# The end of a one-core program: semaphores cleared while the last two stores are in flight, and no release after the clear

## The chip, the cores and the metric

The kernel runs on one core of a Trainium2 chip. A core has five engines that run their own instruction streams: TensorE (PE in the profile), VectorE (DVE), ScalarE (ACT), GpSimd (POOL) and SyncE (SP), and 16 DMA engines that move data between the chip's memory (HBM) and the core's on-chip memory. [...]The number that counts is the device time of one execution in microseconds. It is longer than the span on the profile page, which goes from the first to the last instruction of the program.

## The reference

Two blocks follow each other. The first is a cross-covariance attention over channels, for 4 batches of 6400 tokens with 256 channels; the second is a mixture of 8 low-rank adapters of rank 16, of which each token takes the best two.

```python
qn = q / (norm(q, axis=1) + 1e-6);  kn = k / (norm(k, axis=1) + 1e-6)
a  = softmax(kn.T @ qn / tau)                 # 256 x 256 for each batch
x  = (v @ a).reshape(25600, 256)
logits = x @ w_gate                           # 8 experts
w  = softmax(top2(logits))
out = x + sum over the two experts e of  w_e * (x @ A[e]) @ B[e]
```

## The kernel before

Tokens lie on the 128 partitions, 50 chunks of 128 tokens for each batch. For each batch the kernel first sums the 256x256 matrix `kT q` over all 50 chunks (`do_G`), makes the attention matrix from it, and then goes through the 6400 tokens of `v` in five pieces of ten chunks: transposes, gate logits, the adapter's inner product, and at last the sum `Y` (`do_Y`, lines 955 and 960), which is copied out of the accumulator banks (`do_Ye`, through the copy helper at lines 810 and 812) and stored (`do_store`, line 971).

The order of the instructions on every engine is worked out ahead by a planner (`Plan.run`, with a rank for each step and a simulated clock) and written out as it stands. Loads are issued by GpSimd (line 627), stores by SyncE (line 971). The last two pieces of the last batch are stored in three parts each (`FINE = 2`: four, four and two chunks), so the stores at the end are of 512, 512 and 256 KB, twice. Each store raises one of eight semaphores of SyncE's DMAs by 16 when it is complete; the stores go round these eight in turn. In the built program the store before the last has semaphore 110, the last one has 111, and the one ahead of them 109.

What comes after the last store is the last block of the program, and it is made by the framework, not by the planner. As built and then shortened by `one_end_barrier` (line 487; it edits the list of instructions of that block when the program is finished), it reads:

- SyncE: nine waits (EVENT_SEMAPHORE), each for two semaphores, so that every load, store and engine has come to its last count; then a DRAIN that waits for a tenth and a DRAIN that raises semaphore 96, "gather".
- TensorE, VectorE and ScalarE: a DRAIN that raises semaphore 96, and then a wait for semaphore 97, "release".
- GpSimd: a DRAIN; a wait until semaphore 96 is at four, which takes the four off again; a DRAIN that resets DMA state for the semaphores 99 to 118; one EVENT_SEMAPHORE_RANGE_CLEAR that sets these to zero; a DRAIN; and a raise of semaphore 97 by four, the release.
- All but GpSimd: the wait for semaphore 97, which takes one off, and then the program is over.

All instructions of the block carry line 1030 in the profile, the end of the `with` block that holds the kernel.

Of the kernel before, what the change touches and what calls it, by code (L numbers as in the profile page):

```python
# [486 lines left out]
def one_end_barrier(nc):  # L487


    def trim(nc):  # L490
        end = nc.main_func.blocks[-1]
        ins = list(end.instructions)
        pool = [n for n, i in enumerate(ins) if i.engine == mybir.EngineType.Pool]
        clear = next(n for n in pool if type(ins[n]).__name__ == "InstISA")
        before = [n for n in pool if n < clear and type(ins[n]).__name__ == "InstEventSemaphore"]
        after = [n for n in range(clear + 1, len(ins))]
        release = [n for n in after if n in pool and type(ins[n]).__name__ == "InstEventSemaphore"]
        assert len(before) == 2 and len(release) == 2 and len(after) == 11, (before, release, after)
        drop = {before[-1]} | {n for n in after if n != release[-1] and n != release[0] - 1}
        end.instructions = [i for n, i in enumerate(ins) if n not in drop]  # L500
    nc.at_finalize(trim)


# [1 line left out]
def kernel(  # L505
# [484 lines left out]
    for s in steps:  # L990
        do[s.key[0]](s, *s.key[1:])
        if s.key[0] == "load":
# [3 lines left out]
            if n_load == 4:  # L996
                make_consts()
    first_ahead(nc, {i.ins.name for i in early})
    one_end_barrier(nc)


# [33 lines left out]
```

## Time and profile before

The median of three runs is 254.42 us, the lowest 254.33, the highest 254.62. The profiled run took 254.2 us, with a span of 252.4 us.

| What | before |
|---|---|
| time, us | 254.42 (254.33 to 254.62) |
| span, us | 252.4 |
| TensorE busy | 222.0 us, 88% of the span |
| DMA engines, mean busy share in 38 of the 40 slices | nine tenths or more |
| last matmul ends | about 244.5 us |
| last copy into the output tile | 244.54 to 245.13 us |
| last store issued | 245.15 to 245.65 us |
| last store complete (semaphore 111 at its final count) | 251.51 us |
| last instruction of the program ends | 252.42 us |

The page of the profile gives busy time by engine, the share in 40 slices and the chain of work that ended last. Waits, semaphores, DRAINs and DMA issues are not counted as busy, so the page shows nothing of what happens after the last copy; for that one asks for the instructions of line 1030, for who waited for whom on SyncE, and for the trace's record of single instructions and of semaphore updates with their times. A wait's start in these records is when it was satisfied, not when it began to wait.

### The profile page before, as it was taken

What the parts mean: (1) busy time and instruction counts of PE and PEld (TensorE: products, weight loads), DVE (VectorE), ACT (ScalarE), POOL (GpSimd) and SP (SyncE); (2) the same over time, 40 slices, a digit from 0 to 9 for tenths busy, and PEclk for the clock granted to TensorE, in tenths of its full rate; (3) what the DMA queues carried; (4) which work ended last, traced back from release to release, by engine and by line L of the source; (5) the groups of instructions that cost most, each with busy time, mean ns of one, the idle gap of its engine ahead of it and who ended that gap; (6) DMA issues with size and microseconds to landing.
All of it is one profiled execution on the core that took longest, in us unless ns stands there. A gap on an engine that the chain in (4) does not pass through costs nothing.

```text
span 252.4 us, 6005 instructions
## 1 busy us (share of the span) xinstructions
PE 222.0 (88%) x2467; PEld 196.5 (78%) x2467; DVE 170.8 (68%) x485; ACT 158.1 (63%) x294; POOL 26.8 (11%) x54
## 2 busy tenths in 40 slices
PE   0875995899999899999998997899998989999970
PEld 0463784699899898889996996699977879999960
DVE  0025386179987988777849678869996897598430
ACT  5424223375977758767674778756953958877750
POOL 7003011011000210000102103010000110000000
PEclk9979798599999999999999999999999999999996
DMA  8999999999999999999999999999999999999995
GB/s 255 213 217 209 212 225 210 214 219 216 214 210 235 297 214 220 312 293 235 220 213 314 222 214 218 209 216 210 216 300 407 424 243 300 354 388 430 420 414 219
DMA packets 11147, 66.71 MB, mean 264 GB/s; under 512 B 1264, under 2 KB 1648, under 8 KB 6512
## 3 DMA queue, kind: packets, MB, share of 16 engines
q0 software_dynamic: 6912, 38.80, 74.6%
q1 hardware_dynamic: 3872, 26.87, 25.9%
q10 hardware_dynamic: 336, 0.66, 0.7%
q8 instruction: 19, 0.31, 0.4%
q14 instruction: 8, 0.07, 0.1%
HBM read 78.91 MB, written 26.21 MB: 416 GB/s over the span
## 4 chain that ended last, share of the span: by engine, by line
PE 47%; DMA 37%; DVE 6%; ACT 5%; issue 1%; POOL 0%; POOLq 0%; DVEq 0%
DMA qk<-in_k_dram 25%; PE Y_ps L955 12%; DMA v<-in_v_dram 7%; PE acc L642 7%; PE Y_ps L960 6%; DMA out_dram<-y 5%; PE T_ps L828 5%; PE Z_ps L919 4%; PE gzT_ps L942 4%; PE ZL_ps L852 3%; DVE ssq L670 2%; ACT sq L664 2%; PE acc L646 2%; PE acc L651 2%; PE log_ps L866 1%
## 5 line engine op out<-in xcount | busy, mean ns | idle before, releaser
L642 PE MATMUL acc<-qk 128*128 128x256 bf16 x400 | 74.6, 285 | 14.7 <-DMA qk<-in_k_dram 8.4
L955 PE MATMUL Y_ps<-a_bf,vT 128*128 128x256 bf16 x400 | 60.0, 272 | 0.6 <-ACT y L810 0.6
L670 DVE TENSOR_TENSOR ssq<-ssq,sq 128x1280 f32<-128x1280 f32 (+1 forms) x27 | 43.3, 1603 | 25.3 <-ACT sq L664 25.1
L810 ACT COPY y<-Y_ps 128x512 f32<-128x512 f32 x83 | 47.9, 589 | 18.7 <-PE Y_ps L960 12.0
L664 ACT ACTIVATE sq<-qk 128x1280 f32<-128x1280 bf16 (+1 forms) x27 | 36.9, 1368 | 27.8 <-DVE ssq L670 9.9
L642 PEld LDWEIGHTS <-qk 128*128 128x128 bf16 x400 | 35.8, 103 | 20.3 <-DMA qk<-in_k_dram 10.3
L955 PEld LDWEIGHTS <-vT 128*128 128x128 bf16 x400 | 38.7, 98 | 5.0 <-issue 0.7
L960 PE MATMUL Y_ps<-ball,gzT 128*128 128x256 bf16 x200 | 38.2, 273 | 0.0
L646 PE MATMUL acc<-qk 128*128 128x128 bf16 x210 | 30.4, 227 | 0.0
L651 PE MATMUL acc<-qk 128*128 128x128 bf16 x200 | 28.7, 227 | 0.0
L828 PE MATMUL T_ps<-ident,v 128*128 128x128 f32 x200 | 28.0, 274 | 0.0
L930 DVE TENSOR_TENSOR gz<-Z_ps,gateg 128x256 bf16<-128x256 f32 x60 | 22.4, 439 | 4.2 <-PE Z_ps L919 4.0
L810 ACT COPY vT<-T_ps 128x512 f32<-128x512 f32 (+1 forms) x43 | 21.7, 540 | 5.2 <-PE T_ps L828 4.9
L646 PEld LDWEIGHTS <-qk 128*128 128x128 bf16 x210 | 21.4, 102 | 3.2
L828 PEld LDWEIGHTS T_ps<-ident,v 128*128 128x128 f32 x200 | 21.9, 141 | 0.5
L810 ACT COPY gzT<-gzT_ps 128x256 f32<-128x256 f32 (+1 forms) x45 | 14.7, 348 | 11.9 <-PE gzT_ps L942 11.7
L627 POOL DMA_DIRECT2D v<-in_v_dram x20 | 11.1, 553 | 101.3 <-PE T_ps L828 69.0
L960 PEld LDWEIGHTS <-gzT 128*128 128x128 bf16 x200 | 19.4, 98 | 2.5 <-DVE gzT L812 0.3
L942 PE MATMUL gzT_ps<-ident,gz 128*128 128x128 f32 x100 | 19.7, 281 | 1.4 <-DVE gz L930 1.0
L651 PEld LDWEIGHTS <-qk 128*128 128x128 bf16 x200 | 18.7, 102 | 2.2
L664 ACT ACTIVATE ssq<-qk 128x1536 f32<-128x1536 bf16 x8 | 11.9, 1486 | 9.5 <-DMA qk<-in_k_dram 5.0
L919 PE MATMUL Z_ps<-waA_sb,vT 128*128 128x128 bf16 x240 | 17.7, 219 | 0.0
(80 smaller groups left out, 275.1 us busy)
## 6 DMA issues: line engine op xcount, KB each, us to landing
out_dram<-y SPq DMA_DIRECT2D x18, 1280.0 KB, 13.0
v<-in_v_dram POOLq DMA_DIRECT2D x20, 640.0 KB, 25.6
qk<-in_q_dram POOLq DMA_DIRECT2D x7, 1088.0 KB, 22.9
qk<-in_k_dram POOLq DMA_DIRECT2D x7, 1088.0 KB, 27.5
qk<-in_q_dram POOLq DMA_DIRECT2D x4, 512.0 KB, 23.4
qk<-in_k_dram POOLq DMA_DIRECT2D x4, 512.0 KB, 24.6
qk<-in_q_dram POOLq DMA_DIRECT2D x2, 1024.0 KB, 31.3
qk<-in_k_dram POOLq DMA_DIRECT2D x2, 1024.0 KB, 35.8
```

Of the source, the lines that this page charges most:

```text
L642: nc.tensor.matmul(acc[ic][:, 0:256], kt[:, j, ic::CC], qt[:, j, :], start=c == 0, stop=False, skip_group_check=True)
L646: nc.tensor.matmul(acc[ic][:, 256:384], kt[:, j, ic::CC], kt[:, j, ic::CC], start=False, stop=False, skip_group_check=True)
L651: nc.tensor.matmul(acc[ic][:, 384:512], qt[:, j, ic * P:(ic + 1) * P], qt[:, j, ic * P:(ic + 1) * P], start=False, stop=c == NC - 1, skip_ ...
L664: nc.scalar.activation(out[:, 0:n, :], t[:, j:j + n, :], ACT.Square)
L670: nc.vector.tensor_tensor(out=t, in0=t, in1=held["sq", (w, b, g), ""][:, 0:n, :], op=OP.add)
L810: nc.scalar.copy(out, in_)
L828: nc.tensor.matmul(ps[:, j, :], vt[:, c + j, :].bitcast(FP32), W["ident32"], is_transpose=True, start=(j == 0), stop=(j == n - 1))
L919: nc.tensor.matmul(ps[:, j, :], vT_of(b, i, c + j)[:, :, ic], st[b]["aA"][:, ic, :], start=(j == 0 and ic == 0), stop=(j == n - 1 and ic = ...
L930: nc.vector.tensor_tensor(out=pairs[:, h].rearrange("p c (e r) -> p c e r", e=E), in0=z[:, 2 * h:2 * h + 2, :].rearrange("p c (e r) -> p c ...
L942: nc.tensor.matmul(ps[:, j, :], pairs[:, j * P:(j + 1) * P], W["ident32"], is_transpose=True, start=(j == 0), stop=(j == n // 2 - 1))
L955: nc.tensor.matmul(ps[:, j, :], vT_of(b, i, c + j)[:, :, ic], st[b]["a"][:, ic, :], start=(j == 0 and ic == 0), stop=False, skip_group_che ...
L960: nc.tensor.matmul(ps[:, j, :], pair[:, :, j], W["B"], start=False, stop=(j == 1), skip_group_check=True)
```

## The change

The edit is in `one_end_barrier` alone, so every instruction up to the last store stays as it was. It rebuilds the last block. SyncE's first waits leave out the two semaphores of the last two stores (110 and 111). SyncE then raises the gather semaphore, and only after that waits for 110 and for 111, and takes the count of each off in the same instruction, so that they end at zero. GpSimd's clear is cut into two ranges that leave these two out, 99 to 109 and 112 to 118, each with its DMA reset ahead of it. The release and the waits for it are gone: TensorE, VectorE and ScalarE end after their DRAIN, GpSimd after its second clear. Its purpose is that the clearing lies beside the last two stores instead of behind them.

```diff
+    LATE = 2
+
     def trim(nc):
...
+        copies = [i for i in nc.main_func.blocks[-2].instructions
+                  if i.engine == sp and type(i).__name__ == "InstDMACopy"]
+        late = [i.sync_info.on_update[0].id for i in copies[-LATE:]]
...
+        tail = [step(mybir.InstDrain, sp, [w for w in waits if w.id not in late])]
+        tail += [step(mybir.InstDrain, e, (), signal[e]) for e in signal]
+        for x in late:
+            w = next(w for w in waits if w.id == x)
+            tail.append(step(mybir.InstEventSemaphore, sp, [w], [mybir.SyncUpdate(
+                sync_type="semaphore", id=x, ant_name=w.ant_name, update_mode="sem-sub-imm",
+                update_value=w.wait_value, update_reg=None)]))
+        tail += [ins[[i.engine for i in ins].index(pool)], joined]
...
+        for a, x in spans:
+            n0 = len(end.instructions)
+            nc.gpsimd.dma_reset(range(a, x))
+            nc.gpsimd.sem_clear(range(a, x))
+            tail += list(end.instructions)[n0:]
+        end.instructions = tail
     nc.at_finalize(trim)
```

More of the change, by code (lines that the diff above doesn't have):

```diff
@@ L487, in one_end_barrier @@
 def one_end_barrier(nc):
+    LATE = 2
     def trim(nc):
+        sp, pool = mybir.EngineType.SP, mybir.EngineType.Pool
         end = nc.main_func.blocks[-1]
         ins = list(end.instructions)
[L493 to L500, printed above, removed]
+        copies = [i for i in nc.main_func.blocks[-2].instructions
+                  if i.engine == sp and type(i).__name__ == "InstDMACopy"]
@@ new lines, in trim, with step @@
+        late = [i.sync_info.on_update[0].id for i in copies[-LATE:]]
+        clear = next(n for n, i in enumerate(ins) if type(i).__name__ == "InstISA")
+        lo, hi = ins[clear].ant_dict["range_first"], ins[clear].ant_dict["range_last"]
+        assert len(set(late)) == LATE and all(lo <= x <= hi for x in late)
+        def step(kind, engine, wait=(), update=()):
+            return kind(name=nc.get_next_instruction_name(), engine=engine,
+                        sync_info=mybir.SyncInfo(on_wait=list(wait), on_update=list(update)))
@@ new lines, in trim @@
+        first = next(i for i in ins if i.engine == sp)
+        waits = list(first.sync_info.on_wait)
+        signal = {i.engine: list(i.sync_info.on_update) for i in ins[:clear]
+                  if type(i).__name__ == "InstDrain" and i.engine != pool and i is not first}
+        joined = next(i for i in ins[:clear] if i.engine == pool and type(i).__name__ == "InstEventSemaphore")
+        tail = [step(mybir.InstDrain, sp, [w for w in waits if w.id not in late])]
+        tail += [step(mybir.InstDrain, e, (), signal[e]) for e in signal]
@@ new lines, in trim @@
+        for x in late:
[4 more added lines that the diff above has]
+        tail += [ins[[i.engine for i in ins].index(pool)], joined]
+        spans, a = [], lo
+        for x in sorted(late) + [hi + 1]:
+            if x > a:
+                spans.append((a, x))
+            a = x + 1
```

## The prediction

> **What bounds the end now.** The change touches nothing ahead of the last store, so I read only how the program ends, in four steps. First the slices of the span:
>
> ```profile
> PE   0875995899999899999998997899998989999970
> DMA  8999999999999999999999999999999999999995
> ```
>
> For most of the span both TensorE and the DMA engines are near full; in the last slice (6.3 us) TensorE is idle and DMA is half busy. The last 6 to 7 us belong to stores and to what follows them. The waits of SyncE, over 245.5 to 253 us, say which:
>
> ```profile
> SPq L1030 <- DMA out_dram<-y: 5.6, 5, 2.0
> SPq L1030 <- PEq L1030: 0.5, 1, 0.5
> ```
>
> Columns: waiter, releaser, us in total, times, longest. Five of SyncE's end waits are ended by a store that completes; the sixth, 0.5 us, is a wait at line 1030 itself: SyncE waits for the clear and the release. (The view names PE; by semaphore it is GpSimd's release, 97.) Third, the instructions of line 1030 from 251.45 us to the end: those behind the last store's completion (columns: duration in ns as min/median/max, first and last start):
>
> ```profile
> L1030 SPq EVENT_SEMAPHORE  x5: 17/28/28, 251.5 to 252.4; - x5
> L1030 SPq DRAIN  x2: 7/7/7, 251.8 to 251.8; - x2
> L1030 POOLq EVENT_SEMAPHORE  x2: 17/17/17, 251.9 to 252.3; - x2
> L1030 POOLq DRAIN  x2: 40/66/93, 252.0 to 252.2; - x2
> L1030 POOLq EVENT_SEMAPHORE_RANGE_CLEAR  x1: 139/139/139, 252.1 to 252.1; - x1
> ...
> L1030 PEldq EVENT_SEMAPHORE  x1: 51/51/51, 252.4 to 252.4; - x1
> ```
>
> Last, the same instructions singly, from the trace's records. The semaphore of the last store (111) reaches its count at 251.514. SyncE's wait for it starts at 251.531, then come three more waits (251.592, 251.651, 251.713) and two DRAINs (251.778, 251.836), the second raising the gather at 251.845. GpSimd joins at 251.869, DRAINs at 251.954, clears at 252.076, DRAINs at 252.250, releases at 252.319. SyncE leaves at 252.361 to 252.378, TensorE at 252.424. So **0.91 us of serial bookkeeping stands behind the last landing** (252.424 - 251.514), on the path that sets the end, with nothing beside it.
>
> The time is 254.42, some 2 us beyond the span. Part of it is recorded too: semaphore 2, which the program does not use, gets nine updates from 252.662 to 253.176, nearly all others are reset from 253.079 to 253.740, and nine more updates of semaphore 2 follow from 253.964 to 254.321.
>
> [...]the second chain takes 254.321 - 253.964 = 0.357 us[...]. The first takes 0.514, because one step, the third update, comes 0.196 us after the second instead of 0.038: one engine came late. The reset took 0.66 us here[...]. [...]Here 111 climbs in sixteen steps from 248.04 to 251.51, so its zeroing cannot come earlier than 251.51, and something must still wait for it. [...]the start reported is when the semaphores are satisfied; the trace agrees (landing 251.514, start 251.531), so I may time by starts.
>
> **The change, part by part.**
>
> *Two semaphores taken out of SyncE's first waits.* SyncE no longer stops at 110 (250.894) and 111 (251.531). Its last waiting stop is semaphore 109, satisfied at 249.626, wait started 249.643. Behind it stand, as before behind 111, three satisfied waits and two DRAINs: 251.845 - 251.531 = 0.314 us by the old rows. Gather raised at 249.643 + 0.314 = **249.96**. The other three engines raised theirs by 245.2. Is a DRAIN of SyncE held up by stores in flight? At line 1016 SyncE DRAINs at 0.425 for 131 ns while its load issued at 0.0 lands at 3.95. It is not.
>
> *GpSimd's clear moves forward, and becomes two.* By the old starts: join 249.98, DRAIN with reset 0.085 later, clear 0.122 later, next DRAIN 0.174 later, its clear again 0.122 later and 0.139 long: 0.017 + 0.085 + 0.122 + 0.174 + 0.122 + 0.139 gives an end near **250.62**. This is 0.9 us ahead of the last landing, so the second reset and clear (0.39 us) cost nothing: they lie beside the last two stores. What the trace of before does not show is a reset DRAIN with stores in flight: before, it ran 93 ns with everything landed. From below it is 93 ns. From above, the longest GpSimd DRAIN in the trace waited 13.7 us, from 212.55 to 226.23, for GpSimd's own last load, which landed at 224.24; stores issued at 223.6 and 224.2 were then in flight (they landed at 236.2 and 239.2) and did not hold it.[...] I take 93 ns, and keep the other end in a rival.
>
> *Two waits that zero what they waited for.* The wait for 110 is satisfied at 250.88, for 111 at 251.514. Each is one instruction in place of half of one; GpSimd's join, which also takes a count off, lasts 17 ns, the old two-sided waits 28 ns. Nothing is queued behind them on SyncE but the end of its program. SyncE ends at 251.531 + 0.02 to 0.03 = **251.55**.
>
> *Release and waits for it.* Gone: 252.319 to 252.424, already in the sum. TensorE, VectorE and ScalarE end by 245.2. The span then ends with SyncE: 252.42 - 251.55 = **0.87 us less**, 251.55.
>
> *What the time makes of it.* The end barrier can finish only after SyncE enters it. Before, engines entered at different delays after their last instruction: the first update came 0.24 us after TensorE's end, the second at 252.696, at most 0.31 after ScalarE's; the late third 0.56 after GpSimd's, if that is it. I take 0.28 for SyncE: it enters at 251.83. The other four have entered long before (GpSimd at 250.62 + 0.56 = 251.18), so the delay of 0.16 us in the old chain goes too. Which place SyncE has in the chain no row says. If it is the turning point, fifth of nine, its update moves from 252.959 to 251.83: 1.13 us. If it is the first, the whole chain of 0.357 runs after it and ends at 252.19 instead of 253.176: 0.99. With 0.24 and the turn, 1.17; with 0.56 and the first place, 252.11 + 0.36 = 252.47, 0.71. I choose the turn at 0.28 rounded down: **1.1 us, 254.42 - 1.1 = 253.3**. The bounds give 253.25 to 253.71, and a SyncE that enters faster than any engine of before would give 253.1.
>
> **The rivals.** *The clear still waits for the stores.* If SyncE's or GpSimd's DRAIN is held until the stores in flight are done, the gather or the reset comes at 251.5, and 0.56 us (from the GpSimd DRAIN on) of two resets and clears follow: GpSimd ends near 252.1 instead of 252.34, enters the barrier 0.2 us earlier, and the time is 254.2. For it: no reset under way with stores is shown. Against: the two DRAINs quoted. *What runs after the program takes the gain back.* Something that the trace does not order by the engines' end[...], ends when it did: 254.4, no change. Against it: the first update of semaphore 2 follows TensorE's end by 0.24 us, close enough to be caused by it. *The reset disturbs DMA or waits as long as the DRAIN of before.* That one ended 2.0 us after the load had landed. With the same 2.0 us after the last store, reset DRAINs end at 253.5, and with the clear, second reset and second clear GpSimd ends at 253.9, 1.6 us later than the 252.34 of before: 256.0, slower. Against it: the 93 ns of the reset DRAIN in the trace of before, which itself stood only 0.44 us behind a landing.
>
> **How the numbers follow.** The forecast case has 0.85 (times 253.1 to 253.71), the still-waiting clear 0.06 (254.2), the swallowed gain 0.04 (254.4), the disturbing reset 0.05 (256.0). 0.2% is 0.51 us, so faster means below 253.91: only the first case, 0.85. Same is the second and third, 0.10; slower the last, 0.05. The range takes the first case with the runs' own spread of 0.1 below: 253.0 to 253.75, leaving out the other 0.15.
>
> **What would show each step.** The span should be near 251.55, ended by SyncE at line 1030; two range clears should start near 250.2 and 250.5, before the last completion at about 251.5; no instruction should follow the last SyncE wait. The last copy and last store should not move (244.5 and 245.2). Semaphore 2 should see four updates before 251.5 if SyncE is at the turn. I am wrong if a GpSimd DRAIN at the end is much longer than 0.1 us, if the gather is raised only after 251 us, if the last landing moves by more than 0.3 us, or if the span falls by 0.9 and the time does not.

## The result and the profile after

The changed kernel takes 253.09 us (median of four runs, 252.78 to 253.20), the kernel before 254.51 us in the same comparison: a ratio of 0.9943, 95% interval 0.9926 to 0.996. So 1.42 us less by the medians, where 1.1 was predicted and 253.3 named, inside the range of 253.0 to 253.75.

The slices first. The page of the changed kernel:

```profile
span 250.4 us, 5995 instructions
...
PE   0785995799999899999998999799998989999990
...
DMA  8999999999999999999999999999999999999998
```

The span is 2.0 us shorter, the time only 1.4, and DMA is busier in the last slice, as if the program ended sooner after its stores. Both are partly an artefact. The changed kernel's waits of SyncE on line 44 of the framework's file and the clears, over 244 to 253 us (columns as before: duration in ns, first and last start):

```profile
bacc.py:44 SPq EVENT_SEMAPHORE  x8: 27/28/28, 245.6 to 249.7; - x8
```
```profile
L528 POOLq DRAIN  x2: 66/81/96, 250.0 to 250.2; - x2
```
```profile
L529 POOLq EVENT_SEMAPHORE_RANGE_CLEAR  x2: 68/82/95, 250.1 to 250.3; - x2
```

The last of eight waits of SyncE starts at 249.7, the two resets (DRAINs) and clears run from 250.0 to 250.4, and then nothing: the waits for the last two stores aren't listed. They ran all the same. In the record of semaphore updates, 110 comes to its count at 250.788 and is taken off at 250.822, and 111 at 251.425 and 251.459. The instructions that the edit makes by hand carry no source line, and the page lists only instructions that have one. So the span of 250.4 ends with GpSimd's second clear, some 1.1 us ahead of the program's end, and cannot be compared with 252.4.

What can be compared is the record of updates of semaphore 2 against L, the moment at which the last store's semaphore, 111, is at its final count. (A semaphore is a counter: the last store of the changed kernel raises 111 in sixteen steps, from 247.873 to 251.425, the last 0.33 us after the last packet in the stores' queue ended at 251.091, and SyncE's wait for it takes the count off at 251.459.) Behind the program semaphore 2 gets nine updates, here called the end barrier: in the runs below the third moves with GpSimd's end and the fifth with SyncE's where that is the later, and the ninth comes 0.16 to 0.22 us after the fifth in every profile. Nine more follow, the second barrier:

| us after L (L: before 251.514, after 251.425) | before | after |
|---|---|---|
| first update | 1.148 | -6.847 |
| second | 1.182 | -6.317 |
| third | 1.378 | -0.493 |
| fourth | 1.422 | -0.449 |
| fifth | 1.445 | 0.172 |
| ninth, barrier over | 1.662 | 0.335 |
| ninth of the second barrier | 2.807 | 1.478 |
| device time of the profiled run less L | 2.686 | 1.355 |

The first two updates now follow the DRAINs of TensorE and ScalarE (which raise the gather at 244.347 and 244.953) by 0.23 and 0.16 us; the third, GpSimd's, follows its second clear by 0.535; the fifth waits for SyncE (with SyncE's end 0.85 us later in a run below, it comes 1.21 us later). An engine's update is called its entry into the barrier. (The fourth comes 0.04 after the third in every profile; that it is VectorE's is not shown.) From the ninth update on both kernels take the same: 1.145 and 1.143 us to the end of the second barrier, 0.12 us before which the device time ends. The change is worth 1.662 - 0.335 = **1.33 us** at the barrier and 2.686 - 1.355 = 1.33 us in the time. The other 0.09 of the profiled pair is L itself, which wanders from run to run: it lay between 251.40 and 252.37 in all the profiles below, and the last store took 6.36 to 7.39 us from issue to landing in them.

### The profile page after: what moved, and what is told of

It reads as the page before. It is cut to its first block, busy times and chain, and to the rows that moved or that the text cites. A ratio compares the mean times of both kernels' runs of the same rounds, so it can differ in the third digit from the quotient of the medians.

```text
span 250.4 us, 5995 instructions
## 1 busy us (share of the span) xinstructions
PE 221.4 (88%) x2467; PEld 196.3 (78%) x2467; DVE 171.0 (68%) x485; ACT 157.9 (63%) x294; POOL 26.7 (11%) x54
## 4 chain that ended last, share of the span: by engine, by line
DMA 49%; PE 39%; DVE 4%; ACT 4%; issue 1%; POOL 0%; POOLq 0%; DVEq 0%
DMA qk<-in_k_dram 25%; DMA v<-in_v_dram 18%; PE Y_ps L986 10%; PE acc L673 5%; DMA out_dram<-y 5%; PE Y_ps L991 5%; PE T_ps L859 5%; PE Z_ps L950 3%; PE gzT_ps L973 3%; PE ZL_ps L883 2%; PE acc L682 2%; PE acc L677 2%; DVE ssq L701 1%; PE log_ps L897 1%; ACT sq L695 1%
```

## The experiments

All variants rebuild the last block as the changed kernel does; each also gives the hand-made instructions a source line, so that they show. The edits are printed in short form: in the runs, switches such as `SP_PAD = 16` turn them on. A DRAIN that waits for nothing and raises nothing serves in some of them to take time. The times ahead of a ratio are medians; each ratio is against the kernel before, run beside it. "Barrier over" is the ninth update of semaphore 2.

| run | last end on GpSimd | third update | last end on SyncE | fifth update | barrier over | time less L |
|---|---|---|---|---|---|---|
| before | 0.822 | 1.378 | 0.864 | 1.445 | 1.662 | 2.686 |
| lines only | -1.054 | -0.519 | 0.034 | 0.172 | 0.335 | 1.358 |
| release kept | -0.979 | -0.406 | 0.033 | 0.171 | 0.335 | 1.374 |
| one late store | 0.209 | 0.731 | 0.033 | 0.799 | 1.016 | 2.043 |
| no late store | 0.707 | 1.233 | 0.326 | 1.300 | 1.518 | 2.544 |
| four late stores | -2.934 | -2.405 | 0.033 | 0.169 | 0.331 | 1.351 |
| GpSimd + 6 | -0.674 | -0.137 | 0.034 | 0.174 | 0.337 | 1.367 |
| GpSimd + 16 | -0.052 | 0.485 | 0.033 | 0.552 | 0.770 | 1.794 |
| SyncE + 16 behind | -1.051 | -0.516 | 0.883 | 1.384 | 1.548 | 2.573 |
| SyncE + 4 behind | -1.018 | -0.484 | 0.258 | 0.379 | 0.542 | 1.562 |
| SyncE + 16 ahead | -1.031 | -0.497 | 0.033 | 0.549 | 0.713 | 1.758 |
| GpSimd sits | -0.486 | 0.083 | 0.034 | 0.165 | 0.369 | 1.386 |

All columns are us after that run's own L, from its profile.

Could the edit also have moved L? The median time of a kernel less its last column estimates where the last store landed in its runs: 251.82 to 251.86 for the kernel before run beside them, 251.74 for the changed one, 251.75 to 252.00 for the variants with four runs or more. No shift goes with the number of late stores (251.82 with none, 251.86 with one, 251.75 with four).

**Lines only.** Is the span of 250.4 real?

```diff
-            return kind(name=..., engine=engine, sync_info=...)
+            return kind(name=..., engine=engine, sync_info=..., debug=line)
```

> The changed kernel with one edit: the instructions that it makes by hand carry a source line, so that the profile lists them; nothing else differs. Entry theory (the time is set by the engine that enters the end barrier last, which is now SyncE, 0.14 us after its last wait): same time as the changed kernel, 253.1 us within 0.2, and SyncE's last wait, which the page of the changed kernel did not list, appears at about 251.45 us, 0.02 to 0.03 after the last store's completion, with the span ending there (251.4 to 251.6) and not at 250.4. Rival (the span of 250.4 on the page was real and the program ends with GpSimd's second clear): no wait appears after 250.4.

Measured: 253.36 us, ratio 0.9951 (0.9937 to 0.9965). The time is 0.06 above the range expected, while the barrier ends at the same L + 0.335: by the estimate above, the stores landed later in these runs (252.00). Its SyncE waits at the end, from 251 to 253 us:

```profile
L1075 SPq EVENT_SEMAPHORE  x2: 17/17/17, 251.8 to 252.4; - x2
```

The second of the two starts at 252.4, when the page says the span ends, and 0.017 us after this run's last landing, which came at 252.37, late as L goes; hence the start is not at 251.45. The rival is out. Its clears ended 1.05 us ahead of the landing, as in the changed kernel:

```profile
L535 POOLq EVENT_SEMAPHORE_RANGE_CLEAR  x2: 68/82/95, 251.0 to 251.2; - x2
```

**Release kept.** Does it matter that the release is gone?

```diff
+            tail.append(step(mybir.InstEventSemaphore, pool, (), [... release, "sem-add-imm", 3]))
+            tail += released
```

> The changed kernel with the release put back for TensorE, VectorE and ScalarE: GpSimd raises it by three after its second clear, and these three wait for it before they end. Entry theory: GpSimd and the three are done by about 250.7, long before SyncE at 251.45, so the time stays at that of the changed kernel, 253.1 within 0.15. Rival (the dropped release is a good part of the gain, since four engines waited for it before): 0.1 to 0.5 us slower than the changed kernel, 253.3 to 253.6.

Measured: 253.37 us, ratio 0.9948 (0.9936 to 0.9959), against 253.36 for lines only on the same chip. By the number alone this falls in the rival's range, 0.12 above the one expected; but lines only, which has no release, is as far up, and so it can't speak for the rival. GpSimd's release, here raised by its DRAIN, and the waits for it, from 250.8 to 252 us:

```profile
L1075 POOLq DRAIN  x1: 40/40/40, 250.9 to 250.9; - x1
L1075 ACTq EVENT_SEMAPHORE  x1: 17/17/17, 250.9 to 250.9; - x1
...
L1075 PEldq EVENT_SEMAPHORE  x1: 51/51/51, 250.9 to 250.9; - x1
```

All is over 0.9 us before SyncE's last wait, and the barrier ends at the same L + 0.335. With the clear overlapped, dropping the release is worth nothing.

**One late store.** Is GpSimd's way into the barrier on the path?

```diff
-    LATE = 2
+    LATE = 1
```

> The changed kernel with one late store instead of two: the gather comes after the last store but one. With L for the completion of the last store: that one completes at L - 0.64, gather at L - 0.31, both clears done 0.53 later at L + 0.22, and GpSimd then needs 0.53 to enter the end barrier: L + 0.75, against L + 0.17 for SyncE. Entry theory: GpSimd is again the last to enter, the barrier ends at L + 1.04, against L + 0.34 in the changed kernel and L + 1.66 before: 0.7 us slower than the changed kernel, 253.8, and 0.6 faster than before. Rival (only the end of the program's last instruction counts): the clears end at L + 0.22, 0.19 after SyncE's last wait, so 0.2 slower than the changed kernel, 253.3.

Measured: 253.90 us, ratio 0.997 (0.9958 to 0.9981); the barrier is over at L + 1.016, where 1.04 was expected and the rival's count would give about 0.5. The page shows the clears just around the last landing of this run, 251.54:

```profile
L535 POOLq EVENT_SEMAPHORE_RANGE_CLEAR  x2: 68/82/96, 251.5 to 251.7; - x2
```

They end only 0.18 us after SyncE's last wait, but GpSimd needs another 0.52 us before its update of semaphore 2, and that sets the time.

**No late store.** What is the release worth alone?

```diff
-    LATE = 2
+    LATE = 0
```

> The change without its overlap: no store is late, the clear is one range and lies behind the last store as before, and only the release (GpSimd's DRAIN and raise, and the four waits) is gone. Entry theory: gather at L + 0.33, clear done at L + 0.70, GpSimd enters the end barrier 0.53 later at L + 1.24, and the barrier ends at L + 1.52, against L + 1.66 before: 0.14 us faster than before, 254.35. Rival (end of the last instruction counts): 0.21 faster than before, 254.3, so these two are not told apart by the time but by the barrier's updates in the trace. Second rival (the release is most of the change's gain): 253.6 or less.

Measured: 254.36 us, ratio 0.9994 (0.9986 to 1.0003): the times alone show no difference. The clear lies behind the landing again, at 251.73 in this run:

```profile
L535 POOLq EVENT_SEMAPHORE_RANGE_CLEAR  x1: 139/139/139, 252.3 to 252.3; - x1
```

The barrier is over at L + 1.518 against L + 1.662 before, 0.14 us earlier, as expected. Of this, 0.115 is GpSimd's DRAIN and raise, and 0.03 a shorter way from its last instruction into the barrier. The waits of the other four for the release never were on the path: in the kernel before, TensorE and ScalarE, though freed only by GpSimd's raise, still made the first two updates 0.2 us before GpSimd made the third. The second rival is out.

**Four late stores.** Does more overlap bring more, or disturb the reset?

```diff
-    LATE = 2
+    LATE = 4
```

> The changed kernel with four late stores instead of two: the gather comes after the fifth store from the end, some 3.7 us ahead of the last completion, and SyncE zeroes four semaphores in its own waits. Entry theory: from two late stores on, GpSimd is ahead of SyncE and more overlap brings nothing: barrier end L + 0.335 as with two, 253.1 to 253.4. Rival (more stores in flight make the reset DRAINs slower or hold them back, or an earlier clear brings more): DRAINs over 0.15 us and a later end, or an end below L + 0.3.

Measured: 253.10 us, ratio 0.9938 (0.9922 to 0.9955), barrier over at L + 0.331. The reset DRAINs now run with four and then, after a landing at 248.27, three stores in flight:

```profile
L534 POOLq DRAIN  x2: 66/78/89, 248.1 to 248.3; - x2
```

They take 89 and 66 ns, against 93 with everything landed, more than 3 us ahead of the last landing. They don't wait for SyncE's stores, and no slowing of these shows: the store before the last completes 0.635 us before the last, against 0.63 to 0.65 in all other profiles.

**GpSimd longer by 6 and by 16 DRAINs.** How much slack has GpSimd?

```diff
+        for n in range(6):        # 16 in the second
+            tail.append(step(mybir.InstDrain, pool))
```

> The changed kernel with 6 DRAINs that wait for nothing on GpSimd behind its second clear. One costs 0.07 to 0.095 us by the starts on GpSimd (252.250 to 252.319 before for a DRAIN and what follows), so GpSimd ends 0.42 to 0.57 us later and enters the barrier at L - 0.09 to L + 0.06 instead of L - 0.5. Entry theory: still ahead of SyncE at L + 0.17, so nothing changes: barrier end L + 0.335, 253.1 to 253.4. Rival (GpSimd's end work is on the path at any length): 0.4 to 0.6 us slower.

> The same with 16 DRAINs on GpSimd: it ends 1.1 to 1.5 us later and enters at L + 0.6 to L + 1.0. Entry theory: GpSimd is the last to enter again, the barrier ends 0.284 us after its entry, as before: L + 0.9 to L + 1.3, so 0.55 to 0.95 us slower than the changed kernel, 253.7 to 254.3; GpSimd's third place in the chain shows as a late third update. Rival (the slack behind GpSimd is longer than 0.6 us): no change.

Measured: 253.17 us with 6, ratio 0.9942 (0.9927 to 0.9956), barrier over at L + 0.337; 253.61 us with 16, ratio 0.9956 (0.9941 to 0.9971), barrier over at L + 0.770. The slack behind GpSimd is there and it ends: GpSimd's update at L - 0.137 costs nothing, at L + 0.485 it costs 0.435. The size was missed: one DRAIN takes 0.061 us from start to start and not 0.07 to 0.095, so the 16 took 1.0 us and the effect stayed below the range named. Of the longer version, from 250.8 us on:

```profile
L1075 POOLq DRAIN  x14: 34/34/34, 250.8 to 251.6; - x14
L1075 SPq EVENT_SEMAPHORE  x2: 17/17/17, 251.1 to 251.7; - x2
```

The DRAINs end before SyncE's last wait starts at 251.7, and still GpSimd is the later one in the barrier.

**SyncE longer by 16 DRAINs behind its last wait.** Is SyncE on the path?

```diff
+        for n in range(16):
+            tail.append(step(mybir.InstDrain, sp))
```

> The changed kernel with 16 DRAINs that wait for nothing on SyncE behind its last wait. One costs 0.05 to 0.06 us by the starts of SyncE's two DRAINs (251.778 and 251.836 before; 0.052 apart in the run with lines), so SyncE ends 0.8 to 0.93 us later. Entry theory: SyncE is the last to enter the barrier, so all of it shows: barrier ends at L + 1.15 to L + 1.27 (L: completion of the last store) against L + 0.335, time 253.9 to 254.2, 0.8 to 0.9 above the changed kernel. Rival (the time is fixed by something that does not follow SyncE's end): no change, barrier end at L + 0.34.

Measured: 254.38 us, ratio 0.9994 (0.9986 to 1.0003); barrier over at L + 1.548, 1.21 us later than lines only. So SyncE is on the path with all it does, but by more than expected. The DRAINs took what was predicted (last end at L + 0.883 instead of L + 0.034, 0.85 us):

```profile
L1075 SPq DRAIN  x16: 7/7/7, 252.2 to 253.0; - x16
```

The other 0.36 us came after them: SyncE entered the barrier 0.501 us after its last instruction instead of 0.138. The next three runs ask where that comes from. The sitting theory in them is the author's conjecture from these two figures: that an engine whose last instruction is a wait enters sooner than one that runs up to its end.

**GpSimd made to sit in its last wait; 16 DRAINs ahead of SyncE's last waits; 4 behind.**

```diff
+            if x == late[0]:
+                tail.append(step(mybir.InstEventSemaphore, sp, (), [... release, "sem-add-imm", 1]))
...
+        tail.append(step(mybir.InstEventSemaphore, pool, [release >= 1], [release, "sem-dec"]))
```
```diff
+        for n in range(16):       # ahead of the waits for the last two stores
+            tail.append(step(mybir.InstDrain, sp))
```
```diff
+        for n in range(4):        # behind the last wait
+            tail.append(step(mybir.InstDrain, sp))
```

> The changed kernel, with GpSimd made to sit in a wait as its last instruction: SyncE raises the (otherwise unused) release semaphore by one after it has zeroed the last store but one, at about L - 0.6, and GpSimd waits for that behind its second clear. In question is the time from an engine's last instruction to its entry into the end barrier: 0.14 us for SyncE and 0.15 for ScalarE, 0.23 for TensorE, but 0.54 for GpSimd, and 0.50 for SyncE with 16 DRAINs behind its last wait. Sitting theory[...]: GpSimd enters 0.15 to 0.3 us after its last wait, at L - 0.45 to L - 0.25. Rival (GpSimd's 0.54 is its own): it enters 0.54 after it, at about L - 0.05. The time stays that of the changed kernel in both.

> The changed kernel with 16 DRAINs on SyncE ahead of its two last waits instead of behind them: they take 16 x 0.052 = 0.83 us from L - 1.52, done at about L - 0.69, before the last store but one is complete. Sitting theory: SyncE still sits about 0.6 us in its last wait, so it enters 0.14 after it and the barrier ends at L + 0.335: time as changed. Rival (the number of instructions on SyncE makes the 0.50 us, wherever they stand[...]): entry 0.50 after the last wait, at L + 0.53, barrier end L + 0.69.

> The changed kernel with 4 DRAINs on SyncE behind its last wait instead of 16. Last DRAIN ends at about L + 0.104 + 3 x 0.052 + 0.007 = L + 0.27. [...]the entry is 0.14 later: L + 0.41, barrier end L + 0.57. If any instruction behind the wait loses it, the entry is 0.50 later: L + 0.77, barrier end L + 0.93. Both go by the trace.

Measured, one run each: 253.22, 253.42 and 253.91 us, of which the last has L at 252.35. GpSimd's last wait is satisfied half a microsecond ahead of the landing at 251.83:

```profile
L1084 POOLq EVENT_SEMAPHORE  x1: 17/17/17, 251.3 to 251.3; - x1
```

Freed from it at L - 0.486, GpSimd entered at L + 0.083, 0.569 later: the 0.5 us is its own, whether it sits or runs. (The barrier ended 0.03 us later than in lines only.) With the 16 DRAINs ahead, SyncE sat more than 0.6 us in its last wait and still entered 0.516 after it. Its end, from 250.1 us on:

```profile
L1084 SPq DRAIN  x17: 7/7/7, 250.1 to 251.0; - x17
L1084 SPq EVENT_SEMAPHORE  x2: 17/17/17, 251.0 to 251.7; - x2
```

With 4 behind, it entered 0.121 after the last of them, the first case of what was expected. So the sitting theory falls in both cases that could show it. What stays is that 16 more instructions on SyncE make its entry 0.36 to 0.38 us later, at both places tried, and 4 don't; on GpSimd 16 more leave it as it was (0.537). Why isn't settled: no run shows what SyncE does between its last instruction and its update.

## Why the prediction was right

*The place of the loss.* The gather at 249.96 was measured at 249.87, and against L it is the same to 0.01 us (249.96 is 1.55 us before the 251.514 of before, 249.871 is 1.55 before 251.425). SyncE's last wait at the landing + 0.017 came as predicted (lines only: L + 0.017). Two reset DRAINs of 93 ns each were measured at 96 and 66. The two clears were taken at the old 0.139 each; they took 0.095 and 0.068, for 11 and 7 semaphores instead of 20. With the gather 0.09 earlier, GpSimd ended at 250.40 instead of 250.62. It was no longer on the path.

*The rivals.* The clear that still waits for the stores is refuted by the start of the reset DRAIN at 249.98, 1.4 us ahead of the landing, and by the run with four late stores. The disturbing reset is refuted by the same DRAINs of 66 to 96 ns. That the DRAIN of 13.7 us waited for GpSimd's own last load is the prediction's reading, and no run tests it; shown is that it ends 2.0 us after that load lands, before and after (226.233 against 224.226, 225.923 against 223.921). Why 2.0 us stays open, and nothing here rests on it. The swallowed gain is refuted by the two longer-engine runs: the time follows the last engine into the barrier one for one (SyncE longer by 16: its update 1.21 us later than in lines only, the barrier over 1.21 us later, the time less L 1.22 us more).

*The sum.* The measured 253.09 us lies below the bounds of 253.25 to 253.71 that came from the delays of other engines; it is the case that the prediction put at 253.1, a SyncE that enters faster than any engine seen before. 1.1 was predicted and 1.33 measured with L taken out. SyncE's entry was taken as 0.28 us, from the other engines' 0.24 and 0.31, and is 0.138: 0.14 us. The step from the fifth to the sixth update fell from 0.097 to 0.044 us, 0.05, not foreseen; it is 0.097 or 0.098 in the runs in which GpSimd came last and 0.043 or 0.044 in those in which SyncE clearly did. Rounding 1.13 down took 0.03. These make 1.1 + 0.14 + 0.05 + 0.03 = 1.32. The place of SyncE, chosen as the fifth of nine, was right: four updates stand ahead of it (that the chain turns there is not shown). No row of the profile before told this, so here the choice was in part luck; the first place would have been worth 0.99. The rest of the 1.42 between the medians is within the spread of L.

*One attribution was too coarse.* The prediction put 0.91 us of bookkeeping on the path, up to TensorE's wait for the release, and then a change in the barrier. The path before ran instead from SyncE's gather to GpSimd's clear and raise (L + 0.822) and then 0.556 us to GpSimd's update of semaphore 2. The releases of the others were beside it. The sum came out near because the prediction took the late third update out of the chain as well. And the span of 251.55 was not what the page showed, for the reason of the missing source lines.

## What to carry to other kernels

In this program the end was a path of its own, 1.66 us from the last landing to the end of the barrier, of which 1.33 could go. In another, find which engine enters the end barrier last, counting what it needs after its last instruction, and move everything off that engine that need not follow the last transfer. Here overlapping the clear with two stores (the next to last store completes 1.25 us after the one ahead of it and 0.64 before the last) was enough, one was too few, four brought nothing, and the release mattered only through the engine that sent it (0.14 us). The two spans here, 252.4 and 250.4, could not be compared, because the second left out the last instructions; see that the same instructions are listed in both, and check a span against an event that both must have, such as the last landing.

## What the runs showed of the hardware that was not expected

- From its last instruction to its update in the end barrier GpSimd needs 0.52 to 0.57 us in every profile, SyncE, where it comes last, 0.12 to 0.14 (0.50 and 0.52 in the two runs with 16 more instructions on it), TensorE 0.23 and ScalarE 0.16 in the changed kernel (from their raise of the gather).
- The range clear takes 139 ns for 20 semaphores, 95 for 11, 92 for 9 (four late stores) and 68 for 7.
- A DRAIN that waits for nothing costs about 0.052 us on SyncE and 0.061 on GpSimd from start to start, and neither waited for stores that SyncE had in flight (on SyncE 17 DRAINs of 7 ns from 250.1 to 251.0, SyncE's wait for the last store ending at 251.7; on GpSimd 14 of 34 ns from 250.8 to 251.6, with that wait ending at 251.7).
- With SyncE last and its instructions unchanged, the barrier is over 0.331 to 0.337 us after the last landing in every profile; the scatter of the profiled times is that of the landing itself (251.40 to 252.37 us).
